# Retention attention and a squared-ReLU FFN on one core: decay moved to v and the outputs, undivided w_in loads, one-chunk first blocks

## The chip, the cores and the metric

One core of a Trainium2 chip runs one program. The metric is the device time of that program in microseconds, as the median of the runs. A run is marked slow here when it lies over 1.5% above the fastest of its kernel. The ratios leave these runs out: one of four of the experiment called e14, two of four of e13, and one or two of the runs of the kernel before in two of the calls. The medians and the ranges contain them.

The engines are named as in the profile: PE multiplies matrices, PEld loads its weights, DVE is the vector engine, ACT the scalar engine, POOL the general engine, SP the engine that issues the DMA transfers.

## The reference

```python
# q, k, v: [4, 8, 768, 64] f32 (batch, heads, steps, head size)
gamma = 1 - 2 ** (-5 - arange(8));  scale = 1 / sqrt(64)
for t in range(768):
    state = gamma * state + k[:, :, t] (x) v[:, :, t]        # outer product, one per head
    y[:, :, t] = scale * q[:, :, t] . state
x = y as [3072, 512]                                        # a token's 8 heads side by side
out = relu(x @ w_in) ** 2 @ w_out                           # w_in [512, 2048], w_out [2048, 512]
```

## The kernel before

The tokens are cut into 24 chunks of 128 (six to a batch). A planner in the kernel places every operation on an engine in a fixed order, with durations that its author gave it, so the order of instructions on each engine is set when the kernel is built. It does not adapt to what the chip does.

For each chunk, k, q and v are loaded (256 KB each), converted to bf16 with the decay factors multiplied into q and k on DVE, and transposed on PE. A "visit" on PE then does the values of chunk m and the scores of chunk m + 1. After that come the two FFN products: the first (F1, w_in) for blocks of two or four chunks, the second (F2, w_out) later. The weights arrive in four slices of 1 MB for each matrix and are cast to bf16. The parts:

```python
blocks = [2, 2] + [4] * ((NM - 4) // 4)
NLD, NBF, NQT, NXT, NH2, NWS, NOSB = 6, 4, 3, 4, 3, 4, 3     # NLD: load buffers of q, k, v each
...
def convert(m, x):                       # k and q with a factor on DVE, v a plain copy on ACT
    if x == "v":
        pl.add(f"cv{m}", "ACT", 0.6, ..., lambda: nc.scalar.activation(o[:], t[:], AF.Copy), ...)
    else:
        pl.add(f"c{x}{m}", "DVE", 0.72, ..., lambda: nc.vector.tensor_tensor(
            out=o[:], in0=t[:], in1=f[:, i, :, None].to_broadcast([P, H, D]), op=ALU.mult), ...)
...
orient = lambda p, hh: hh if p < 2 else 1 - hh               # heads of pairs 2, 3 sit in exchanged halves
...
def weights(kind, j, parts):
    def fn():
        if kind == "in":                 # one slice of w_in in three DMAs
            wv = moe_w_in.rearrange("(cb p) f -> p cb f", p=P)[:, :, j * 512 : (j + 1) * 512]
            nc.sync.dma_start(st[:, 0:2, :], wv[:, 0:2, :])              # 512 KB, all 128 partitions
            nc.sync.dma_start(st[0:64, 2:4, :], wv[64:128, 2:4, :])      # 256 KB, 64 partitions
            nc.sync.dma_start(st[64:128, 2:4, :], wv[0:64, 2:4, :])      # 256 KB, 64 partitions
        else:                            # one slice of w_out in one DMA
            wv = moe_w_out.rearrange("(fb p) n -> p fb n", p=P)
            nc.sync.dma_start(st[:], wv[:, 4 * j : 4 * j + 4, :])
...
# order of the loads: chunks 0, 1; w_in 0, 1; chunk 2; w_in 2; chunk 3; w_in 3; w_out 0, 1; ...
```

The exchanged halves of `orient` are why a w_in slice took three transfers: rows of w_in had to follow the heads.

## Time and profile before

| | before |
|---|---|
| median of 3 runs | 244.16 us (241.3 to 244.72) |
| span of the profiled run | 241.8 us |
| PE busy | 204.9 us (85%) |
| DVE, ACT, POOL busy | 107.2, 125.7, 12.0 us |
| first FFN matmul starts | 27.04 us |
| last load (v of chunk 23) lands | 127.4 us |

The profile's page of the kernel before, part 1 (busy time), part 2 (40 slices of about 6 us each; digits are tenths of busy time, the last row is what the DMA engines moved) and part 4 (who the chain of waits runs through):

```profile
PE 204.9 (85%) x2469; PEld 110.3 (46%) x2496; DVE 107.2 (44%) x248; ACT 125.7 (52%) x219; POOL 12.0 (5%) x24
...
PE   1503696885879999998999999999999999999994
...
DMA  7998999999999999999982011111100111111112
GB/s 155 251 248 181 207 223 216 216 266 269 280 270 214 205 211 226 230 207 204 251 212 77 3 43 43 43 46 43 43 18 28 43 43 43 43 46 45 61 69 87
...
PE 51%; DMA 25%; SPq 13%; DVE 7%; issue 1%; ACT 1%; POOL 1%; ACTq 0%; POOLq 0%
```

The DMA row is full for 20 slices, and PE has gaps only there. From about 130 us on the loads are over and PE is full. So there are two stages: the first is set by the loads, the second by PE.

The first FFN matmul, and the last waits of PE for a load, as the timeline and the chain of waits of before have them (start, duration, what):

```profile
27.04 3.57 PE L423 MATMUL fps<-xt,w_in 128*128 128x256 bf16 x16 [2.41 <-ACT xt L381]
...
238.34 0.60 ACT L466 ACTIVATE osb<-fps 128x512 f32<-128x512 f32 x1 [2.86 <-PE fps L457]
```

```profile
117.89 5.30 DMA qn<-in_q_dram
123.21 0.69 DVE qs L256
```

The last load on the chain is the q of chunk 22, which lands at 123.2 us. From its conversion at 123.21 us to the last copy of an output at 238.34 us lie 115.13 us, nearly all PE work in a fixed order.

### The profile page before, as it was taken

Reading aid. Unit: us, or ns where it says so; the run is one execution under the profiler, and the core shown is the slowest. Engines: PE = TensorE matmul, PEld = TensorE weight load, DVE = VectorE, ACT = ScalarE, POOL = GpSimd, SP = SyncE. Lnnn points to the kernel's source line nnn. Section 1 sums busy time; section 2 is a strip of 40 time slices with the busy share of each in tenths; the row PEclk is TensorE's granted clock in tenths of the full one; section 3 lists DMA queues with packets and bytes.
Section 4 is the critical chain, followed back from the end, with each engine's and each line's share of the span. In section 5 each row is a group of like instructions: output and inputs, shape, how many; then the busy total and the mean of one; then the engine's idle time right before and its main releaser. Section 6 shows DMA issues by size and latency. Waiting matters only on the chain.

```text
span 241.8 us, 5820 instructions
## 1 busy us (share of the span) xinstructions
PE 204.9 (85%) x2469; PEld 110.3 (46%) x2496; DVE 107.2 (44%) x248; ACT 125.7 (52%) x219; POOL 12.0 (5%) x24
## 2 busy tenths in 40 slices
PE   1503696885879999998999999999999999999994
PEld 0402474664434555555555544444444444444441
DVE  3443455778349768876966322222222222221000
ACT  2522373886548998576869533444444344442110
POOL 2011102004202000000000000000000000000000
PEclk9999997999999999999999999999999999999998
DMA  7998999999999999999982011111100111111112
GB/s 155 251 248 181 207 223 216 216 266 269 280 270 214 205 211 226 230 207 204 251 212 77 3 43 43 43 46 43 43 18 28 43 43 43 43 46 45 61 69 87
DMA packets 82713, 33.92 MB, mean 140 GB/s; under 512 B 75520, under 2 KB 75520, under 8 KB 82688
## 3 DMA queue, kind: packets, MB, share of 16 engines
q1 hardware_dynamic: 82688, 33.56, 59.9%
q8 instruction: 19, 0.31, 0.6%
q14 instruction: 6, 0.05, 0.1%
HBM read 27.26 MB, written 6.29 MB: 139 GB/s over the span
## 4 chain that ended last, share of the span: by engine, by line
PE 51%; DMA 25%; SPq 13%; DVE 7%; issue 1%; ACT 1%; POOL 1%; ACTq 0%; POOLq 0%
PE fps L457 28%; PE fps L423 21%; SPq L243 9%; DMA qn<-in_q_dram 6%; DMA wst<-in_moe_w_out_dram 6%; DMA kn<-in_k_dram 5%; DMA vn<-in_v_dram 4%; DMA wst<-in_moe_w_in_dram 3%; DVE h L431 2%; SPq L394 2%; DVE state L374 2%; DVE qs L256 1%; DVE pt L359 1%; DVE ks L256 1%; SPq L395 1%
## 5 line engine op out<-in xcount | busy, mean ns | idle before, releaser
L423 PE MATMUL fps<-xt,w_in 128*128 128x512 bf16 (+1 forms) x434 | 99.4, 359 | 7.1 <-ACT xt L381 2.6
L457 PE MATMUL fps<-w_out,h 128*128 128x512 bf16 x371 | 93.7, 379 | 1.5 <-POOL w_out L406 0.6
L428 ACT ACTIVATE h<-fps 128x512 bf16<-128x512 f32 (+1 forms) x112 | 58.7, 536 | 54.6 <-PE fps L423 52.9
L431 DVE TENSOR_TENSOR h<-h 128x512 bf16<-128x512 bf16 (+1 forms) x112 | 43.1, 396 | 74.9 <-ACT h L428 74.9
L423 PEld LDWEIGHTS <-w_in 128*128 128x128 bf16 x448 | 44.4, 102 | 44.5 <-issue 4.3
L457 PEld LDWEIGHTS <-h 128*128 128x128 bf16 x384 | 37.1, 98 | 43.2 <-issue 1.1
L252 ACT ACTIVATE vs<-vn 128x512 bf16<-128x512 f32 x24 | 15.0, 628 | 24.6 <-DMA vn<-in_v_dram 24.6
L271 ACT ACTIVATE qkT<-tp 128x1024 bf16<-128x1024 bf16 x24 | 24.5, 1022 | 1.8 <-PE tp L267 1.6
L466 ACT ACTIVATE osb<-fps 128x512 f32<-128x512 f32 x24 | 14.3, 598 | 18.3 <-PE fps L457 18.3
L267 PE MATMUL tp<-ident,ks 128*128 128x128 bf16 x96 | 10.5, 239 | 15.1 <-DVE ks L256 14.4
L256 DVE TENSOR_TENSOR ks<-kn,kf 128x512 bf16<-128x512 f32 x24 | 16.9, 704 | 13.3 <-DMA kn<-in_k_dram 13.3
L256 DVE TENSOR_TENSOR qs<-qn,qf 128x512 bf16<-128x512 f32 x24 | 16.5, 686 | 5.1 <-DMA qn<-in_q_dram 4.8
L374 DVE TENSOR_TENSOR state<-sc,state 128x256 bf16<-128x256 f32 x40 | 16.7, 417 | 0.6
L359 DVE TENSOR_TENSOR pt<-sc,cmask 128x512 bf16<-128x512 f32 x24 | 16.4, 683 | 0.4 <-PE sc L337 0.4
L381 ACT ACTIVATE xt<-yy 128x512 bf16<-128x512 f32 x24 | 14.2, 591 | 3.9 <-PE yy L312 3.4
L267 PEld LDWEIGHTS <-ks 128*128 128x128 bf16 x96 | 6.8, 106 | 18.3 <-DVE ks L256 16.4
L325 PE MATMUL sc<-qkT 64*64 64x64 bf16 x384 | 7.8, 201 | 7.7 <-ACT qkT L271 4.9
L312 PE MATMUL yy<-qkT,state 64*64 64x64 bf16 x352 | 12.4, 199 | 0.1
L267 PE MATMUL tp<-ident,qs 128*128 128x128 bf16 x96 | 10.2, 234 | 1.2 <-DVE qs L256 1.2
L325 PEld LDWEIGHTS <-qkT 64*64 64x64 bf16 x384 | 5.6, 113 | 8.9 <-ACT qkT L271 5.8
L296 PEld LDWEIGHTS <-vs 64*64 64x64 bf16 x384 | 5.4, 110 | 8.5 <-issue 4.5
L267 PEld LDWEIGHTS <-qs 128*128 128x128 bf16 x96 | 6.9, 105 | 3.5 <-DVE qs L256 2.5
(26 smaller groups left out, 54.5 us busy)
## 6 DMA issues: line engine op xcount, KB each, us to landing
kn<-in_k_dram SPq DMA_DIRECT2D x24, 256.0 KB, 5.2
qn<-in_q_dram SPq DMA_DIRECT2D x24, 256.0 KB, 5.4
vn<-in_v_dram SPq DMA_DIRECT2D x24, 256.0 KB, 5.3
out_dram<-osb SPq DMA_DIRECT2D x24, 256.0 KB, 2.0
wst<-in_moe_w_out_dram SPq DMA_DIRECT2D x4, 1024.0 KB, 7.4
wst<-in_moe_w_in_dram SPq DMA_DIRECT2D x4, 512.0 KB, 6.8
wst<-in_moe_w_in_dram SPq DMA_DIRECT2D x8, 256.0 KB, 7.2
```

What stands on the lines that cost most here:

```text
L243: nc.sync.dma_start(ld[x][m % NLD][:], src[x][b, :, i * C : (i + 1) * C, :].rearrange("h s d -> s h d"))
L252: lambda: nc.scalar.activation(o[:], t[:], AF.Copy), prio=m)
L256: lambda: nc.vector.tensor_tensor(out=o[:], in0=t[:], in1=f[:, i, :, None].to_broadcast([P, H, D]), op=ALU.mult),
L267: nc.tensor.transpose(tp[:, half, p, :], s[:, 2 * p : 2 * p + 2, :], ident[:])
L271: lambda: nc.scalar.activation(qkT[:], tp[:], AF.Copy), prio=m - 0.5)
L359: lambda: nc.vector.tensor_tensor(out=pt[:], in0=sc[:, :, 0:256].rearrange("s g (p t) -> s g p t", p=NP), in1=cmask[:, None, None, :].to_b ...
L374: lambda cc=cc, j1=j1, j0=j0: nc.vector.tensor_tensor(out=sts[j1][:], in0=cc, in1=sts[j0][:], op=ALU.add), prio=n - 0.55)
L423: nc.tensor.matmul(ps[:, :n], lhsT=w_in_bf[j][:, cb, c * P : (c + 1) * P], rhs=xt[:, cb, :n], start=(cb == 0), stop=(cb == NCB - 1))
L428: nc.scalar.activation(h2[:, fb, :n], ps[:, :n], AF.Relu)
L431: nc.vector.tensor_mul(h2[:, fb, :n], h2[:, fb, :n], h2[:, fb, :n])
L457: nc.tensor.matmul(ps[:], lhsT=h2[:, fb, q4 * C : q4 * C + C], rhs=w_out_bf[j][:, c, :], start=(fb == 0), stop=(fb == NFB - 1))
L466: nc.scalar.activation(osbs[slot][:], fps[o1["op"]["bank_index"]][:], AF.Copy)
```

## The change

Its intent is to let FFN work start earlier and to relieve ACT.

- The decay factors leave q and k. They go to v (one product on DVE) and to the outputs (a table `yf`, one product on DVE instead of a copy on ACT). q and k become casts, for which the planner may choose an engine; it chose POOL for all 48.
- `orient` goes, so each w_in slice is loaded by one DMA over all partitions.
- Blocks are 1, 1, 1, 1, 1, 1, 2, 4, 4, 4, 4 chunks; the matmuls of a one-chunk block have 128 columns, four F1 groups share a bank.
- Before chunk 6 a visit does scores alone or values alone.
- The loads come in another order (w_in slices between the chunks, w_out earlier), with five load buffers in place of six.

The core of the diff, cut:

```diff
-    LAND = 0.6
+    LAND = 1.25
...
+BLOCKS = [1, 1, 1, 1, 1, 1, 2, 4, 4, 4, 4]
+SPLIT = 6
+F2LAG = 5.0
+CAST = {"k": {"DVE": 0.43, "ACT": 0.63, "POOL": 0.78}, "q": {"DVE": 0.43, "ACT": 0.63, "POOL": 0.78}}
...
+ORDER = "c0 c1 i0 c2 i1 c3 i2 i3 c4 o0 c5 o1 o2 o3"
...
-    NLD, NBF, NQT, NXT, NH2, NWS, NOSB = 6, 4, 3, 4, 3, 4, 3
+    NLD, NBF, NQT, NXT, NH2, NWS, NOSB, NST = 5, 4, 3, 4, 3, 4, 3, 6
...
-            pl.add(f"c{x}{m}", "DVE", 0.72, (f"ld{x}{m % NLD}", f"{x}f"), (f"bf{x}{m % NBF}",), ...   # product
+            pl.add(f"c{x}{m}", CAST[x], 0, (f"ld{x}{m % NLD}",), (f"bf{x}{m % NBF}",), ...            # cast
...
-            pl.add(f"Y{m}", "ACT", 0.62, ("yy",), ...                                                 # copy
+            pl.add(f"Y{m}", "DVE", 0.68, ("yy", "yf"), ...                                            # product with yf
...
-                nc.sync.dma_start(st[:, 0:2, :], wv[:, 0:2, :])
-                nc.sync.dma_start(st[0:64, 2:4, :], wv[64:128, 2:4, :])
-                nc.sync.dma_start(st[64:128, 2:4, :], wv[0:64, 2:4, :])
+        pl.add(f"ldw{kind}{j}", "SP", 2.75, (), (f"wst{slot}",),
+               lambda: nc.sync.dma_start(st[:], wv), prio=dma_prio[(kind, j)])
...
+        if m + 1 < NM and m + 1 < SPLIT:
+            if m >= 0:
+                visit(m, None)
+            visit(None, m + 1)
+        else:
+            visit(m if m >= 0 else None, m + 1 if m + 1 < NM else None)
```

## The prediction

> **What bounds it now.** Two things in sequence. The DMA row is full until about 127 us (share 1.0 or more in every 10 us window), then nearly idle. Stretches that carry only q, k and v move 206 to 208 GB/s (80 to 90 and 100 to 110 us), one with weights 289 (50 to 60 us). The Trainium skill, "DMA: Bandwidth & Descriptors", section "Why small descriptors are slow", gives 256-byte pieces a 27% overhead; this trace agrees in direction. After 140 us PE is 99.5% busy (79.63 of 80 us); four 128x512 matmuls take 0.86 us. The chain of waits is DMA and SyncE with short DVE steps until about 124 us, then PE matmuls alone.
>
> PE's own work, from counts in the instruction order and spacings in the timeline (0.2157 us per 512-column matmul, 0.117 per 256, 0.057 per transpose, 0.65 per visit), is an estimated 193 us. So about 45 us of the 241.8 us span are lost, nearly all before 75 us: the first FFN matmul starts at 27.0 us although the first w_in slice landed at 13.2 us, because it needs chunk 1, computed with chunk 2's scores. The last w_out slice lands at 72.6 us with an estimated 160 us of PE work behind it.
>
> **What changes.** One-chunk blocks and separate scores/values let FFN1 start when chunk 0 and the first w_in slice are there, about 14 us. w_out slices come earlier in the DMA order. 128-column matmuls cost an estimated 0.062 us each, so PE's work rises to about 196 us. By the new order PE does 39.6 us of work before the last w_out slice (33.5 before), 92 before chunk 23's transposes (86), and has 89 left at its values (102). The k and q products (0.70 us each on DVE) become casts, and all 48 go to POOL (0.78 us each for the weights' casts). v's product and y's scaling move from ACT (0.63, 0.59 us) to DVE (about 0.69 each), so DVE's total hardly changes and ACT is relieved. Neither is the limit. The Trainium skill, "SBUF — State Buffer", section "SBUF: two separate sides", says a POOL op and a two-SBUF-input DVE op lock each other out; the trace agrees (squares of 0.34 to 0.43 us take 0.7 to 0.8 beside POOL casts). I expect about 0.4 us more DVE per chunk, absorbed.
>
> **Critical path after.** Bytes are unchanged, so the loads still end at 127 to 129 us, two stores more being queued before the last one. So part of the early gain becomes waiting for chunks. Chunk 23's q lands at about 127 us, plus a cast, plus 103.5 us of PE work: PE ends at about 231 to 233 (238.3 before). With the same 3.5 us tail and 1.8 us from span to time: **237.3 us, 80% range 233.5 to 241.5**. Chances: faster by over 2% 0.60, within 2% 0.36, slower by over 2% 0.04.
>
> **What the profile would show.** First FFN1 matmul at 13 to 16 us; DMA full until 126 to 130 us; PE's waits shifted from the first 75 us into 75 to 128 us, on q/k casts and on DVE; POOL busy about 50 us; ACT down by 20 to 25 us; the chain of waits: loads of the last chunks, then PE.
>
> **What would make it wrong.** POOL casts well over 1 us, or DVE locked out so that visits trail the loads by several us (near 243). DVE blocking in order on late v loads. Loads ending before 126 us (whole-partition slices moving faster): under 234.

## The result, and the profile after

| | before | after |
|---|---|---|
| median | 244.44 us (4 runs, 241.3 to 244.74) | 232.83 us (4 runs, 232.06 to 233.45) |
| span of the profiled run | 241.8 us | 231.7 us |
| PE, DVE, ACT, POOL busy | 204.9, 107.2, 125.7, 12.0 us | 205.2, 111.5, 104.8, 38.9 us |
| first FFN matmul | 27.04 us | 15.96 us |
| fourth w_in slice complete | 37.4 us | 31.2 us |
| q, v of chunk 23 land | 126.5, 127.4 us | 123.2, 126.0 us |

The kernel is faster by 4.5%: the ratio is 0.9551, with a 95% interval of 0.9467 to 0.9635. A ratio here is the mean time of one kernel's fast runs over that of the other's in the same rounds, so it is not quite the ratio of the medians. The predicted 237.3 us, and the range down to 233.5, were too high.

The same parts of the page of the kernel after (40 slices of 5.8 us):

```profile
PE 205.2 (89%) x2725; PEld 120.4 (52%) x2752; DVE 111.5 (48%) x244; ACT 104.8 (45%) x160; POOL 38.9 (17%) x67
...
PE   1556999778699999989979999999999999999993
...
DMA  7999998998999999999897011001111101111212
GB/s 152 261 198 294 348 216 187 279 270 187 357 198 223 207 240 221 194 237 203 195 212 203 0 48 45 26 22 45 45 45 48 38 8 45 45 48 45 91 45 91
...
PE 66%; DMA 20%; SPq 6%; DVE 2%; ACT 2%; issue 1%; POOL 1%; POOLq 0%; ACTq 0%
```

The DMA row looks as before, full until about 126 us. But in two of its early slices (17 to 29 us) it now moves 294 and 348 GB/s. The timeline and the chain of waits of the kernel after, at the places shown of before:

```profile
15.96 1.89 PE L462 MATMUL fps<-xt,w_in 128*128 128x128 bf16 x16
...
228.19 0.60 ACT L504 ACTIVATE osb<-fps 128x512 f32<-128x512 f32 x1 [2.86 <-PE fps L496]
```

```profile
111.88 6.92 DMA kn<-in_k_dram
118.94 0.62 POOL ks L287
```

The conversions of chunk 23's q and v, which wait for their loads alone, show when these land:

```profile
123.33 0.61 POOL L287 CAST qs<-qn 128x512 bf16<-128x512 f32 x1 [1.54 <-DMA qn<-in_q_dram]
...
125.99 0.69 DVE L305 TENSOR_TENSOR vs<-vn,vf 128x512 bf16<-128x512 f32 x1 [1.00 <-DMA vn<-in_v_dram]
```

Now the last load on the chain is the k of chunk 22, cast at 118.94 us; from there to the last copy are 109.25 us. So the end came 10.15 us earlier (238.34 to 228.19), of which 4.27 us are the chain's last load converted earlier (123.21 to 118.94) and 5.88 us less work behind it (the two loads are not the same tensor, so this split is rough). Had that k landed as late as I had put the last chunk's q (127 us, 3.8 us later than it did), the same arithmetic would give an estimated 118.94 + 3.8 + 109.25 = 232.0 us for the last copy and, with the tail of 3.5 us and 1.8 us from span to time, 237.3 us. That is the prediction. So by this estimate its sum held in everything but the landing.

Why did the loads land earlier with "bytes unchanged"? The first suspect is the only thing that changed in the transfers themselves, the undivided w_in slices.

### The profile page after: what moved, and what is told of

Same layout as the page of the kernel before. It is cut to its first block, busy times and chain, and to the rows that moved or that the text cites. A ratio compares the mean times of both kernels' runs of the same rounds, so it can differ in the third digit from the quotient of the medians.

```text
span 231.7 us, 6304 instructions
## 1 busy us (share of the span) xinstructions
PE 205.2 (89%) x2725; PEld 120.4 (52%) x2752; DVE 111.5 (48%) x244; ACT 104.8 (45%) x160; POOL 38.9 (17%) x67
## 4 chain that ended last, share of the span: by engine, by line
PE 66%; DMA 20%; SPq 6%; DVE 2%; ACT 2%; issue 1%; POOL 1%; POOLq 0%; ACTq 0%
PE fps L496 31%; PE fps L462 28%; DMA wst<-in_moe_w_out_dram 10%; SPq L295 6%; DMA kn<-in_k_dram 5%; DMA wst<-in_moe_w_in_dram 3%; DMA qn<-in_q_dram 2%; PE tp L316 2%; PE yy L330 2%; PE yy L345 1%; PE sc L356 1%; PE sc L367 1%; DVE xt L424 1%; ACT h L467 1%; ACT osb L504 1%
## 5 line engine op out<-in xcount | busy, mean ns | idle before, releaser
L462 PE MATMUL fps<-xt,w_in 128*128 128x128 bf16 (+2 forms) x693 | 99.5, 289 | 2.1 <-DVE xt L424 0.7
L467 ACT ACTIVATE h<-fps 128x512 bf16<-128x512 f32 x96 | 57.2, 596 | 73.2 <-PE fps L462 71.7
L472 DVE TENSOR_TENSOR h<-h 128x512 bf16<-128x512 bf16 x96 | 42.1, 445 | 67.6 <-ACT h L467 67.3
L462 PEld LDWEIGHTS <-w_in 128*128 128x128 bf16 x704 | 55.3, 102 | 31.6 <-issue 1.5
L305 DVE TENSOR_TENSOR vs<-vn,vf 128x512 bf16<-128x512 f32 x24 | 16.9, 705 | 14.0 <-DMA vn<-in_v_dram 14.0
L287 POOL CAST ks<-kn 128x512 bf16<-128x512 f32 x24 | 15.0, 627 | 40.5 <-DMA kn<-in_k_dram 23.9
L424 DVE TENSOR_TENSOR xt<-yy,yf 128x512 bf16<-128x512 f32 x24 | 16.5, 686 | 7.9 <-PE yy L345 7.9
L287 POOL CAST qs<-qn 128x512 bf16<-128x512 f32 x24 | 15.0, 626 | 15.8 <-DMA qn<-in_q_dram 15.8
L345 PEld LDWEIGHTS <-state 64*64 64x64 bf16 x352 | 7.7, 109 | 5.2 <-DVE state L415 2.0
```

The costliest lines, as they stand in the source:

```text
L287: nc.gpsimd.tensor_copy(o, t)
L305: lambda: nc.vector.tensor_tensor(out=o[:], in0=t[:], in1=vf[:, i, :, None].to_broadcast([P, H, D]), op=ALU.mult),
L345: nc.tensor.matmul(yy[L * c : L * c + L, sub, p * L : p * L + L], lhsT=st[r, j, :], rhs=qkT[r, 1, j, sub * L : sub * L + L], start=False, ...
L424: lambda: nc.vector.tensor_tensor(out=xt[:, :, u * C : u * C + C].rearrange("s p (g t) -> s g p t", g=2), in0=yy[:, :, 0:256].rearrange("s ...
L462: nc.tensor.matmul(ps[:, u * n : u * n + n], lhsT=w_in_bf[j][:, cb, c * P : (c + 1) * P], rhs=xt[:, cb, cols], start=(cb == 0), stop=(cb = ...
L467: nc.scalar.activation(h2[:, f0 : f0 + per, cols], ps[:].rearrange("p (u n) -> p u n", u=per), AF.Relu)
```

## The experiments

All ran with three rounds of timing, thus four runs each. "Its before" is the kernel before, run on the same chip. Landing times are read from the completion events in the trace, in the time of the views (the same landings stand 0.1 to 0.2 us later in some of the expectations).

### e1: the kernel after, w_in slices in three transfers again

```diff
-        pl.add(f"ldw{kind}{j}", "SP", 2.75, ..., lambda: nc.sync.dma_start(st[:], wv), ...)
+            if kind == "in":
+                nc.sync.dma_start(st[:, 0:2, :], wv[:, 0:2, :])
+                nc.sync.dma_start(st[0:64, 2:4, :], wv[0:64, 2:4, :])
+                nc.sync.dma_start(st[64:128, 2:4, :], wv[64:128, 2:4, :])
+            else:
+                nc.sync.dma_start(st[:], wv)
```

The planner sees the same duration, so the order on every engine is that of the kernel after.

> The changed kernel, but each w_in slice is loaded in three DMAs again (all partitions 0.5 MB, lower half 0.25 MB, upper half 0.25 MB, straight, so the result stays right). PE's order is the same instruction for instruction. Theory A (the loads pace PE: PE ends when chunk 23's q lands plus what the order has left behind it, 103.7 us, and the three-part slices take 5 to 6 us each against 3.3 to 4.2 whole): the fourth w_in slice lands at 36 to 38 us instead of 31.3, chunk 23's q 2.5 to 4 us later than 123.3, time 235.5 to 237.5 us. Theory B (the gain is the earlier FFN of small blocks; the slices' form does not matter): time within 1 us of the changed kernel, 232 to 233.8.

Measured: 239.5 us (239.15 to 242.33), its before 243.11, ratio 0.991 (0.983 to 0.999). The division costs 6.7 us of the median, more than I expected. In the profiled run the fourth slice is complete at 40.4 us instead of 31.2, and chunk 23's q lands at 132.0 instead of 123.2. The chain of waits of e1, and in its timeline the cast of chunk 23's q and the last copy:

```profile
121.62 6.03 DMA kn<-in_k_dram
127.80 0.62 POOL ks L287
```

```profile
132.08 0.61 POOL L287 CAST qs<-qn 128x512 bf16<-128x512 f32 x1 [1.48 <-DMA qn<-in_q_dram]
...
237.05 0.60 ACT L511 ACTIVATE osb<-fps 128x512 f32<-128x512 f32 x1 [2.86 <-PE fps L503]
```

237.05 - 127.80 = 109.25 us, to the hundredth what the kernel after needs. PE's work behind the load did not change at all; the whole loss is the landing.

### e2: the kernel before, w_in slices in one transfer

```diff
-                nc.sync.dma_start(st[:, 0:2, :], wv[:, 0:2, :])
-                nc.sync.dma_start(st[0:64, 2:4, :], wv[64:128, 2:4, :])
-                nc.sync.dma_start(st[64:128, 2:4, :], wv[0:64, 2:4, :])
+                nc.sync.dma_start(st[:], wv)
```

Its result is wrong: the old order of heads needs the exchanged halves. The instructions and the sizes of everything are the same; that other values leave the times alone is assumed.

> The kernel before with each w_in slice in one DMA over all partitions (the halves of two of four row blocks are then not exchanged, so the result is WRONG on purpose; the instructions and their order on every compute engine are the same). Theory A: the fourth w_in slice lands about 6 us earlier than 37.4, the last w_out slice 3 to 6 us earlier than 72.6, and the time falls by 2.5 to 5 us, to 239 to 242. Theory B: within 1 us of before, 243.5 to 245.

Measured: 236.63 us (234.72 to 238.13), ratio to its before 0.9787 (0.970 to 0.988), again more gain than I expected. Fourth slice at 28.7 us, chunk 23's q at 117.3, v at 118.1. The chain of waits and the timeline of e2:

```profile
108.92 5.41 DMA qn<-in_q_dram
114.35 0.69 DVE qs L256
```

```profile
229.47 0.60 ACT L464 ACTIVATE osb<-fps 128x512 f32<-128x512 f32 x1 [2.86 <-PE fps L455]
```

229.47 - 114.35 = 115.12 us; the kernel before had 115.13. Again only the landing moved.

The two experiments complete a square. Medians first (the kernel before had 242.1 to 244.4 us), then the time of the last copy and of chunk 23's q and v in the profiled runs:

| | w_in in three transfers | w_in in one |
|---|---|---|
| old order | 243.1 us; copy 238.34; q 126.5, v 127.4 | 236.6 us; copy 229.47; q 117.3, v 118.1 |
| new order | 239.5 us; copy 237.05; q 132.0, v 135.0 | 232.8 us; copy 228.19; q 123.2, v 126.0 |

One transfer for a slice is worth 6.5 us by the medians in the old order and 6.7 in the new one, and 8.9 us in the profiled runs in either. All the rest of the change is worth 3.6 to 3.8 us by the medians (1.3 us in the profiled runs). This is the surprise: the loads of the new order are by themselves later, in the profiled runs by 5.5 to 5.9 us (q: 117.3 to 123.2, or 126.5 to 132.0), and the undivided slices hid it. My "loads still end at 127 to 129 us" was near the measured 126.0 us by luck: two terms that I had not put in at their size, about +8 and -9 us for the last v, cancel.

A profiled run is one run, and two of these were not typical: e1's is the slowest of its four (242.33 us), e2's the fastest (234.72 us). So the 8.9 us, and the landings read from these traces, probably overstate what the division costs; the medians are the better measure. The ratios to before differ by 2.1% in the old order and 3.6% in the new (about 5 and 9 us), each ratio with an interval of nearly 1% either way. That the division costs time in both orders is shown; that it costs the same in both is not.

Where in time the transfers are lost is seen in the windows of 16 to 48 us of four kernels. Columns: stretch, its length, busy time and instructions of PE, PEld, DVE, ACT, POOL, then the granted clock, the DMA engines' busy share, GB/s. The kernel before:

```profile
16.00:48.00 32.00, 19.86 (x366) 15.26 (x367) 17.62 (x43) 16.26 (x34) 3.99 (x6) 0.95 1.12 210
```

e2, the kernel before with undivided slices:

```profile
16.00:48.00 32.00, 24.11 (x488) 19.08 (x489) 21.18 (x52) 20.86 (x45) 3.38 (x6) 0.95 1.09 266
```

e1, the new order with divided slices:

```profile
16.00:48.00 32.00, 22.67 (x425) 20.39 (x424) 14.38 (x32) 12.88 (x21) 7.08 (x10) 0.84 0.99 192
```

The kernel after:

```profile
16.00:48.00 32.00, 26.77 (x612) 24.52 (x608) 22.34 (x44) 17.50 (x27) 9.80 (x14) 0.95 1.04 257
```

The busy share is about 1 in all four, but the kernels with divided slices move 210 and 192 GB/s where those with undivided ones move 266 and 257. (The stretch holds loads of q, k and v too, and after 39 us, in the two quicker ones, w_out. Counted to the landing of the fourth slice alone, where each has moved 7.6 to 7.9 MB, the traces give 211 GB/s for before and 196 for e1, against 265 for e2 and 253 for after.) The clock granted to PE was low in this stretch of e1 (0.84), but e2 and before had the same 0.95.

### e10: is it the number of transfers or the half of the partitions?

```diff
-        ... nc.sync.dma_start(st[:], wv) ...
+                nc.sync.dma_start(st[:, 0:2, :], wv[:, 0:2, :])
+                nc.sync.dma_start(st[:, 2:3, :], wv[:, 2:3, :])
+                nc.sync.dma_start(st[:, 3:4, :], wv[:, 3:4, :])
```

Three transfers of the same sizes as in e1 (512, 256 and 256 KB), but each over all 128 partitions.

> The changed kernel with each w_in slice in three DMAs of the same sizes as in the three-part run (0.5, 0.25, 0.25 MB), but every one over all 128 partitions; descriptors stay 2 KB. Theory H (what costs time is that two of the parts reach only half of the partitions): fourth w_in slice at 30 to 33 us, time 232 to 234, like the changed kernel. Theory N (the number of DMAs, or their smaller size, costs the time): fourth slice at 37 to 41 us, time 237.5 to 240.5, like the three-part run.

Measured: 233.04 us (232.12 to 233.8), its before 243.66, ratio 0.9564 (0.951 to 0.962): the same as the kernel after. Slice four is complete at 31.1 us, chunk 23's q lands at 123.6. From chunk 22's k cast (in the chain of waits) to the last copy (in the timeline) are again 228.45 - 119.20 = 109.25 us:

```profile
119.20 0.63 POOL ks L287
```

```profile
228.45 0.60 ACT L511 ACTIVATE osb<-fps 128x512 f32<-128x512 f32 x1 [2.86 <-PE fps L503]
```

So it is not the number of transfers; it is the two that reach only half of the partitions. A cast that waited for the fourth slice's last part, in the timelines of after, of e1 and of e10, in this order:

```profile
31.25 0.87 POOL L287 CAST w_in<-wst 128x512 bf16<-128x512 f32 x1 [2.64 <-DMA wst<-in_moe_w_in_dram]
```

```profile
40.45 0.43 DVE L285 CAST w_in<-wst 128x512 bf16<-128x512 f32 x1 [2.06 <-DMA wst<-in_moe_w_in_dram]
```

```profile
31.12 0.43 DVE L285 CAST w_in<-wst 128x512 bf16<-128x512 f32 x1 [0.98 <-DMA wst<-in_moe_w_in_dram]
```

The Trainium skill says this: "SBUF — State Buffer", section "Door 1: The DMA port swizzle", has partitions 0 to 63 reach 8 of 16 ports, with 196 GB/s measured at 1 MiB where 128 partitions gave 328; and its section "Can I just issue two DMAs to hit both halves?" answers no, two transfers to the two halves serialize. These runs agree in direction, with the numbers above.

### e14: the kernel after, w_in and w_out slices divided

```diff
-            if kind == "in":        # of e1
+            if True:
```

> The three-part run (239.5 us) with the w_out slices in three parts as well, two of them over half of the partitions: twice the suspected cost, PE's order unchanged. If half-partition parts cost the time: the loads end another 5 to 9 us later, time 244 to 249. If only the early slices matter (because they delay the FFN's start): 239 to 241.

Measured: 245.04 us (242.48 to 246.2; 244.58 without the slow run), its before 242.1, ratio 1.008 (0.996 to 1.020): the whole gain of the change is gone. As expected in time. But in the profiled runs chunk 23's q lands at 134.3 us, only 2.3 us later than in e1 (the last copy at 239.32 against 237.05), where I had expected 5 to 9 us and the four divided w_in slices had cost 8.8. This does not show that w_out's division costs less: e1's profiled run was the slowest of its four. By the medians of the fast runs w_out's division costs 5.1 us (244.58 against 239.5) and w_in's 6.7; by the ratios 1.7% and 3.6%, each difference uncertain by over 1%. Whether the two differ is open. The chain of waits and the timeline of e14:

```profile
123.88 6.04 DMA kn<-in_k_dram
130.07 0.62 POOL ks L287
```

```profile
239.32 0.60 ACT L511 ACTIVATE osb<-fps 128x512 f32<-128x512 f32 x1 [2.86 <-PE fps L503]
```

239.32 - 130.07 = 109.25 us for the third time.

### e15: why the new order loads later

The new kernel has five load buffers each for q, k and v, the old one six. Six of all three do not fit, so q and k get six here and v keeps five.

```diff
-    NLD, NBF, ... = 5, 4, ...
+    NLD, NBF, ... = 6, 4, ...
-    ld = {x: [sb(f"{x}n{j}", [P, H, D], FP32) for j in range(NLD)] for x in "qkv"}
+    ld = {x: [sb(f"{x}n{j}", [P, H, D], FP32) for j in range(NLD - (x == "v"))] for x in "qkv"}
```

> The kernel after, with six load buffers for q and k in place of five (v keeps five; six of all three do not fit). Why: with the same form of weight DMAs the new order lands the last chunks about 6 us later than the old one (chunk 23's q at 123.3 us against 117.5 in the kernel before with whole slices; 132.1 against 126.5 with slices in three parts). Theory B: the loads wait for free buffers, since the new kernel has five of each and the old one six. Then chunk 23's q lands at 119.5 to 121.5 us and the time is 229.5 to 231.5. Rival S: it is the two more stores queued ahead of the last loads (512 KB, about 2.3 us at 220 GB/s) and DMA engines idling for other reasons; then chunk 23's q stays within 1 us of 123.3 and the time within 1.2 us of 232.8.

Measured: 231.92 us (229.44 to 232.36), its before 243.2, ratio 0.9539 (0.942 to 0.966). Chunk 23's q landed at 118.8 us, even before the stretch that theory B named, but the time came out in the rival's range, not in B's. The order of the loads, which the planner changed with the buffers, fits both: q and k now run ahead and the v's come last (chunk 23's at 123.6 us), and v is on the chain of waits, where this is the last load:

```profile
116.42 5.07 DMA vn<-in_v_dram
```

The last load of all lands at 123.6 us instead of 126.0. So the missing buffers cost about 2.4 us of the 7.8 us by which the new order's last v is late, and hardly anything of the time. Two more stores ahead of the last load (five instead of three, 512 KB, an estimated 2.4 us at 220 GB/s) are a second part. The remaining 3 us or so are open, and may be nothing but the scatter of single runs: e2's profiled run was 1.9 us under its median, and that of after 0.6 us over its own. If that lay in the landings, the new order's loads would be later by an estimated 2.5 us less than the profiled runs say.

### e4: the old blocks in the new kernel

```diff
-BLOCKS = [1, 1, 1, 1, 1, 1, 2, 4, 4, 4, 4]
+BLOCKS = [2, 2, 4, 4, 4, 4, 4]
```

> The changed kernel with the FFN's blocks of before, 2, 2 and then 4 chunks; all else as changed. PE's total work falls by an estimated 2.6 us, but the order leaves 111.5 us of work behind chunk 23's transposes instead of 103.7. Theory A: the loads land as in the changed kernel, so the end moves by that difference, +6 to +8 us: 238.5 to 241. Theory B (earlier start of the FFN is worth what PE gains before 75 us, about 10 us) expects about 242 to 244. If small blocks were worth nothing: 230 to 233.

Measured: 239.08 us (238.47 to 240.17), its before 243.11, ratio 0.987 (0.981 to 0.993). The small blocks are worth about 6 us. The loads end earlier here (chunk 23's q at 119.7 us, with four stores ahead of the last load instead of five), and yet the time is longer: more PE work is left. From chunk 23's k transposes to the last copy lie 113.0 us, against 104.8 in the kernel after. Blocks and loads seem to pull against each other, since FFN work done early finishes outputs early, whose stores queue with the loads; no run tested this alone.

### e3: scores and values together from the second chunk on

```diff
-SPLIT = 6
+SPLIT = 1
```

> The changed kernel with scores and values in joint visits from chunk 1 on, as in the kernel before, instead of apart until chunk 6. The order leaves the same work behind every late chunk (103.7 us behind chunk 23's transposes). Theory A (the late loads pace PE): 231.8 to 234, although the first FFN matmul of chunk 0 and 1 may come several us later. If the separate scores and values are worth what they gain at the start: 234.5 to 237.

Measured: 231.94 us (231.82 to 232.49), its before 243.66, ratio 0.9528 (0.947 to 0.959). Separate visits are worth nothing, though the prediction named them as a reason for the early start. The first FFN matmul starts at 13.83 us without them, and from chunk 22's k cast to the last copy are 109.24 us.

### e5 and e12: is POOL the right engine for the casts?

e5 lets q and k be cast on DVE alone. e12 keeps what the planner then makes of the order and issues those same casts on POOL.

```diff
-CAST = {"k": {"DVE": 0.43, "ACT": 0.63, "POOL": 0.78}, "q": {"DVE": 0.43, "ACT": 0.63, "POOL": 0.78}}
+CAST = {"k": {"DVE": 0.43}, "q": {"DVE": 0.43}}
# e12, besides:
-                   lambda on, t=t, o=o: copy_on(on, ...
+                   lambda on, t=t, o=o: copy_on("POOL", ...
```

> The changed kernel with all 48 casts of q and k on DVE instead of POOL (DVE plus 48 times 0.43 us, 20 us more, POOL down by 30 us). The planner, seeing DVE fuller, leaves 95.3 us behind chunk 23's transposes instead of 103.7. If DVE keeps up, the loads pace less and PE ends 3 to 5 us earlier: 228 to 230.5. If DVE becomes the pace of the load stage (busy over 95% from 70 to 125 us), visits trail the loads and the time is 233 to 240. I expect the second, about 235, with less certainty than for the others.

Measured: 227.76 us (227.45 to 228.14), its before 243.66, ratio 0.9349 (0.930 to 0.940). I missed it widely. DVE was not saturated: it was busy 53.90 of the 64 us from 64 to 128 us, which is 84%, and PE 62.17 of 64.

> The run with q's and k's casts on DVE (227.8 us), in exactly its order on PE and SyncE, but with these 48 casts issued on POOL. So it differs from that run in the engine of the casts alone, and from the changed kernel in the order alone. If the order made that run faster (95.3 us left behind chunk 23 instead of 103.7) and POOL's casts are as good as DVE's: 227 to 229. If POOL's casts (0.61 to 0.89 us, locking with DVE) were what held the changed kernel back: 231 to 233. I expect the first.

Measured: 228.83 us (227.99 to 229.69), its before 242.1, ratio 0.9453 (0.939 to 0.952). So by the medians 4.0 of e5's 5.1 us are the order that the planner found and 1.1 the engine (0.6 us by the last copies of the two profiled runs). By the ratios to before, taken on different chips, it is about half and half (1.0% each). Both play a part; how much each is not settled. From chunk 23's k transposes to the last copy there are 96.2 us in e5 and in e12, against 104.8 in the kernel after: more FFN work was done before the loads ended. The windows of 64 to 128 us of the kernel after, of e5 and of e12, in this order (columns as above):

```profile
64.00:128.00 64.00, 60.59 (x1139) 36.84 (x1152) 46.23 (x92) 34.38 (x49) 19.07 (x31) 0.98 0.96 210
```

```profile
64.00:128.00 64.00, 62.17 (x1148) 36.87 (x1159) 53.90 (x123) 34.09 (x51) 0.00 (x0) 1.00 0.93 208
```

```profile
64.00:128.00 64.00, 64.00 (x1172) 38.26 (x1171) 47.05 (x94) 34.63 (x51) 20.40 (x30) 1.00 0.95 205
```

PE loses 3.4 us in this stretch of the kernel after and nothing in that of e12.

### e8, e11 and e13: a slower plan of the loads

If the order leaves too little FFN work in the load stage because the planner believes the loads are quick, a slower belief should help. e8 gives the planner longer transfers; the transfers themselves are the same. e13 is e8 with e5's casts. e11 goes further and coarsens the blocks.

```diff
-            pl.add(f"ld{x}{m}", "SP", 1.17, ...
+            pl.add(f"ld{x}{m}", "SP", 1.27, ...
-        pl.add(f"ldw{kind}{j}", "SP", 2.75, ...
+        pl.add(f"ldw{kind}{j}", "SP", 3.4, ...
# e11: 1.35 and 3.6, and
-BLOCKS = [1, 1, 1, 1, 1, 1, 2, 4, 4, 4, 4]
+BLOCKS = [1, 1, 2, 2, 2, 4, 4, 4, 4]
```

> The changed kernel with only the planner's two DMA durations raised to what the trace shows (1.27 us per q, k or v tile instead of 1.17, 3.4 us per weight slice instead of 2.75), so that more FFN work is ordered ahead of the late chunks: 97.8 us left behind chunk 23's transposes instead of 103.7. Theory A: PE ends 3 to 6 us earlier as long as the loads land as before: 227.5 to 230.5 us. If the loads do not pace PE and PE's own work does, nothing is gained: 232 to 233.5.

Measured: 228.72 us (226.95 to 229.89), its before 243.11, ratio 0.9434 (0.936 to 0.951), in the expected range. The chain of waits on the page of e8:

```profile
PE 88%; ACT 3%; DMA 2%; issue 2%; DVE 2%; SPq 1%; POOL 0%; ACTq 0%
```

The loads are off the chain, 2% against 20%. PE is what remains.

> The run with the planner's slower DMA durations, carried further (1.35 us per tile, 3.6 us per weight slice) and with fewer one-chunk blocks (1, 1, 2, 2, 2, then 4s), which takes an estimated 1 us off PE's work. From the landings of that run no load should pace PE after the last w_out slice; the rest is PE's own work. Theory A: 226 to 229 us, at least as fast as that run (228.7). If later starts or DVE make it lag: over 230.

Measured: 231.02 us (229.75 to 232.26), its before 243.66, ratio 0.9482 (0.941 to 0.955). A miss. The wait view of e11 has PE waiting for ACT's and DVE's steps of the visits:

```profile
PE sc L356 <- ACT qkT L320: 5.8, 5, 1.4
...
PE yy L330 <- DVE pt L402: 3.2, 5, 0.8
```

In e8 these are 3.8 and 1.6 us. But the profiled runs of e8 and e11 have the same span (228.0 and 227.9 us), so what makes the other runs of e11 slower is not shown.

> Casts of q and k on DVE and the planner's slower DMA durations (1.27 and 3.4 us) together: 90.3 us left behind chunk 23's transposes. From the landings of the DVE run the loads no longer pace PE after the last w_out slice, so what is left is PE's own work and its waits of the first 64 us: 226 to 229, hardly better than either alone.

Measured: 228.4 us (226.13 to 230.33), its before 242.1, ratio 0.9357 (0.927 to 0.945): as expected hardly better than either alone. Its two runs that are not marked slow took 226.13 and 226.9 us. By the median the best correct version is e5 at 227.76 us, with e13 (nearly the same ratio to before) and e8 within the scatter.

## Why the prediction was wrong, and where it was right

**The step that failed** is the one that the prediction put as "Bytes are unchanged, so the loads still end at 127 to 129 us" and "Chunk 23's q lands at about 127 us". That q landed at 123.2 us. The bytes were unchanged and the rate was not. Two of the three transfers of a w_in slice reached 64 partitions, and with undivided slices 257 GB/s were moved where divided ones gave 192 in the same order and stretch (e1). In the profiled runs this lands chunk 23's q 9.2 us earlier in the old order (e2) and 8.8 in the new. Against it stands a second term that I had sized too small: the new order's own loads are nearly 6 us later (e2 to after), of which I had counted only two stores. The difference of 9.2 and 5.9 is the 3.3 us by which this q landed ahead of the one before; it beat my 127 us by 3.8. (By the medians the first term is nearer to 6.6 us, and the second then an estimated 3.3 us; their difference stays.) The rest of the sum then gives 237.3 us, as shown above, so this is the term that was mis-sized, and the mechanism (a load, then a fixed amount of PE work) was right: 109.25 us in four kernels of the new order (after, e1, e10, e14), 115.13 and 115.12 in two of the old.

I had written down the cause among the things that would make it wrong, "whole-partition slices moving faster", and given it no part of the sum. With the landing falls the step built on it, "part of the early gain becomes waiting for chunks": up to 75 us PE was not busy for 30.2 us in the kernel before and for 19.0 us in that after; from 75 to 128 us it was not busy for 2.3 and 3.1 us. Of 11.1 us gained early only 0.8 became waiting.

The one rate of weights that the prediction names, 289 GB/s, is from a stretch of the profile in which w_out slices came, already undivided. And I read the landing of a slice's first transfer (the cast on DVE at 13.18 us) as the slice's, which was complete only at 15.3 us. These two lines of the timeline of before show it, the same slice by its first part and by its last:

```profile
13.18 0.43 DVE L404 CAST w_in<-wst 128x512 bf16<-128x512 f32 x1 [2.10 <-DMA wst<-in_moe_w_in_dram]
...
15.33 0.43 DVE L404 CAST w_in<-wst 128x512 bf16<-128x512 f32 x1 [1.73 <-DMA wst<-in_moe_w_in_dram]
```

A clue was on the page as well: the DMA row stood at 9 with 207 to 223 GB/s from 24 to 42 us, when the third and fourth w_in slices came, and at 9 with 266 to 280 GB/s from 48 to 72 us, when w_out came (q, k and v were loaded in both). It is not a clean one, as the first two w_in slices came with 248 to 251 GB/s (6 to 18 us). The Trainium skill, "Perfetto Trace Analysis", section "Identifying the Most-Contended Engine", warns that with 16 DMA engines occupancy misleads, and has the use of HBM's bandwidth looked at instead; this trace agrees, with 204 to 280 GB/s under the same 9.

Point by point:

- *Two stages, loads then PE*: right. PE was busy 79.63 of 80 us after 140 us in both kernels.
- *First FFN matmul at 13 to 16 us*: right, 15.96 us. The reason was half wrong: separate scores and values were not needed for it (e3).
- *DMA full until 126 to 130 us*: right to the eye, at 126.0 us, by two errors that cancel.
- *The last w_out slice*: it landed at 64.5 us, before at 72.6.
- *POOL busy about 50 us*: 38.9. A cast of q or k took 0.63 us on average, not the 0.78 us that I had taken from the casts of weights.
- *ACT down by 20 to 25 us*: right, 125.7 to 104.8.
- *PE's work behind chunk 23's transposes falls to about 103.5 us*: right in size; from its k transposes to the last copy are 104.8 us, before 108.4.
- *DVE locked out by POOL, absorbed*: the first is right. The Trainium skill, "SBUF — State Buffer", section "SBUF: two separate sides", has the exclusive lock; squares in 64 to 128 us took 470 ns on average, against 434 before and 418 with no casts on POOL (e5). That it was wholly absorbed is not shown: e12 against e5 puts the whole cost of POOL for the casts at 1.1 us by the medians and 1.0% by the ratios.
- *PE's waits move to 75 to 128 us*: right in kind, as 2.3 of the 3.1 us lost there are waits for casts of q and k, but hardly any of the early gain was lost there (above).

## What to carry to other kernels

When a change alters the shape of transfers, cost the transfers anew, by their own landing times and GB/s from the trace, even if the bytes stay the same; a full DMA row says only that the engines are occupied. Keep transfers over all 128 partitions, and if the layout forces halves, change the layout. And with a fixed order per engine, write the end as one landing plus the work behind it: that sum was exact to a hundredth of a microsecond over six kernels here, so an error must be in the landing or in the order, and both can be read.

## What the Trainium skill lacked or had wrong

- "SBUF — State Buffer", section "Door 1: The DMA port swizzle", gives the rate of a transfer over 64 partitions alone, not what it does to the queue behind it. In e1 four divided slices (half of whose bytes went over 64 partitions) delayed everything after them: the fourth slice by 9.2 us (31.2 to 40.4), chunk 23's q by 8.8 us (123.2 to 132.0), with many 128-partition loads in between. Next to nothing was caught up later in this trace, of a run 2.8 us slower than the median of e1; by the medians the four slices cost 6.7 us of the time.
- "GPSIMD Engine Reference" has POOL about twice as slow as DVE for two-input elementwise work and calls one-input work roughly line-rate. The f32 to bf16 cast of 128x512 took 0.61 us on POOL at its quickest (after) and up to 1.15 (e4), against 0.42 us on DVE (e5), so at this size POOL is slower by about 45% at best here. Whether that is a rate or a fixed cost of each instruction, no run shows.
